# Row maxima of both heads together from the first slot on, and a new order of issue, in an attention and FFN kernel

## The chip, the cores and the metric

The kernel runs on one core of a Trainium2 chip. The metric is the device time of one execution in microseconds, the median of several runs. Below, PE is the matmul engine (TensorE), DVE the vector engine, ACT the scalar engine, POOL the GpSimd engine and SP the engine that issues all DMAs here.

## The reference

Queries, keys and values have 4 batches, 8 heads, 768 tokens and 64 columns. Each query and key is hashed to 6 bits, the signs of its products with `proj`; a query sees the keys with the same bits. The attention's output, 3072 tokens of 512 columns, goes through a feed-forward layer with 2048 hidden columns.

```python
q_bits = (np.einsum('bhsd,dk->bhsk', q, proj) > 0).astype(np.int64)
k_bits = (np.einsum('bhsd,dk->bhsk', k, proj) > 0).astype(np.int64)
...
mask = q_bucket[:, :, :, None] == k_bucket[:, :, None, :]
scores = scale * np.matmul(q, k.transpose(0, 1, 3, 2))
scores = np.where(mask, scores, -1000000000.0)
scores = scores - np.max(scores, axis=-1, keepdims=True)
attn = np.exp(scores)
attn = attn / (np.sum(attn, axis=-1, keepdims=True) + 1e-09)
return np.matmul(attn, v).astype(np.float32)
...
h = x @ w_in
sp = np.where(h > 20.0, h, np.log1p(np.exp(np.minimum(h, 20.0))))
g = h * np.tanh(sp)
return (g @ w_out).astype(np.float32)
```

## The kernel before

**Units and slots.** The work is cut into 12 units of 256 tokens, three to a batch. A unit's attention has 8 slots: four pairs of heads, and for each pair two chunks of 128 queries. There are 96 slots. Slot n makes the scores of two heads (128 queries by 768 keys each), and its steps are:

- *Scores* (`att_front`, line 841): matmuls of a slice of QT with KT into `ps_s`, a PSUM tile of 128 x 1536, 768 columns for each head. Two sums add up: one over the high halves, one over the low halves together with the hash bits, which are scaled so that keys of another bucket come out far below the others. The operations are called S, and T for the second head where heads are apart.
- *Row maximum* (line 846): DVE reduces the scores, and two small instructions (lines 850 and 853) make the scale and the bias of the exponential from it.
- *Exponential* (`att_exp`, line 873): one ACT instruction for each head, from `ps_s` into one of three buffers `pb`; it also sums the row.
- *Back* (`att_back`): the sums' reciprocal (lines 897, 903). In the first unit, PE multiplies the exponentials by a diagonal matrix (`pe_turn`, line 435), which scales and transposes them in one step, and ACT or DVE copies the result to PT (line 438). In later units the scaled exponentials are split in a high and a low float16 half (lines 366 to 369, 387, 393, 394) and transposed by DMA (line 447).
- *Output* (`att_pv`): after every second slot, PT times VT into `ps_t` (line 950 in the first unit, 939 later), and a copy to X.

**The feed-forward layer.** Each unit has 8 pieces of 256 hidden columns: H (line 985 in the first unit, 995 to 997 later), the activation on ACT (lines 1012 and 1016), a split in halves, and two matmul groups O for the two chunks of 128 tokens (line 1034, later 1044 to 1046). It trails the attention by 12 slots (`LAG`), so that the first H follows slot 10's scores. Until then the program is in its lead-in: attention of the first unit and of three slots of the second, and what prepares it.

**Preparation.** Loads of q, k, v and weights are issued by SP (line 443). Squares of them are summed on ACT (line 455) and over partitions on PE (lines 471, 472), which gives a power of two to scale by; the scaled values are split in halves, transposed by DMA (line 447) into QT and KT, hashed by PE (line 705) and DVE (lines 709, 713), and transposed again with the bits. Weights arrive as 64-bit words in a few staging regions and are brought to float32 by four steps a piece (`w_prep`: `w_u`, `w_sign`, `w_low`, `w_join`, the last at line 580).

**What sets the order.** `Plan` records every operation with the engines that could do it. The string `ORDER` names all of them by number, in the order in which they are issued, and a letter picks the engine where there is a choice. Each engine works through its own operations in that order, and waits for whatever it reads or overwrites. `BACKBONE` sets the order in which operations are numbered.

**By head.** In slots 0 to 8 (`n < BY_HEAD`, with `BY_HEAD` 9) scores and maxima are separate operations for each head: S and a maximum over one head, T and a maximum over the other. From slot 9 on, one operation S makes both heads' scores, and one reduction makes both maxima.

Of the kernel before, what the change touches and what calls it, by code (L numbers as in the profile page):

```python
# [87 lines left out]
13 7 12 6 50 15 48 52 4 34 3 97 144 77 0 1 2 20 8 17 16 14 54 53 5 21 22 35b 18 19 25 37 23c 26 9 10 11 24c 61  # L88
62 63 89 107 98c 108 99b 38 58 59 60 109c 64 27 28 36 65 66 39 29 145b 110 30 87 40 49 41 31 32 42 90 100 43
44 146 78 79c 51 46 33 147 111 67 68 69 70 163 164 165 71 72 166b 167 168 80b 45 93 91 94 92 96 95 116c 373b  # L90
55 101 81 82 126 154 83 84 214c 88 85 73 117 118 127 124 102 56 114 57 103 203c 155b 121b 119 122 74 156b 125
104 157 105 75 129 204b 128 120 130d 131 132 148 86 140 141 115 138 149 150 169 47 106 123 133 230b 143 112
185 139 134 142 183 113 151 186 205 135 231b 359 162 136 175d 176 177 184 232b 360 178 361 233 206 137 187 158
161 179 188 264b 197 212 189c 198 152 190 191c 194c 180b 213 362b 253 207 234 199 215 200 192 202 181 201 170
226 364 171 172 173 238 153 211 237 174 210 159 224 193b 182 216d 254b 255 217 218b 221b 195 225 227 160 228
196 304b 305b 219 247 222 208 248 229 239c 220 249 240 297 241c 209 244 280 315 251 306b 242 274 262 250 256
252 266d 275 307 267 257 223 281b 263 243 282b 276 277 245 235 278 246 271 268 269 236 308 279 270 289c 283
# [12 lines left out]
600 611 606 612d 622b 594 613 607 561 614 582 633 623 629 627 635 624b 583 584 630b 636 671 667 637 593 585  # L110
# [105 lines left out]

# [971 lines left out]
```

## Time and profile before

| | us |
|---|---|
| median of 3 runs | 870.38 (868.37 to 870.57) |
| the profiled execution | 869.01 |
| its span, first to last instruction | 867.2 |
| first scores start | 29.61 |
| scores of slot 9 start | 105.10 |
| first matmul of the feed-forward layer | 115.08 |
| last matmul ends | 863.4 |

All times on the trace count from the span's start. A row of a timeline gives start, duration, engine, line, instruction, what it writes and reads, how many instructions were merged, and in brackets how long its engine had been idle before it and what released it. A row of a group gives the count, then total busy time and the mean in ns of one, then the idle time before them.

### The profile page before, as it was taken

Reading aid. Unit: us, or ns where it says so; the run is one execution under the profiler, and the core shown is the slowest. Engines: PE = TensorE matmul, PEld = TensorE weight load, DVE = VectorE, ACT = ScalarE, POOL = GpSimd, SP = SyncE. Lnnn points to the kernel's source line nnn. Section 1 sums busy time; section 2 is a strip of 40 time slices with the busy share of each in tenths; the row PEclk is TensorE's granted clock in tenths of the full one; section 3 lists DMA queues with packets and bytes.
Section 4 is the critical chain, followed back from the end, with each engine's and each line's share of the span. In section 5 each row is a group of like instructions: output and inputs, shape, how many; then the busy total and the mean of one; then the engine's idle time right before and its main releaser. Section 6 shows DMA issues by size and latency. Waiting matters only on the chain. (4 is left out here: it accounts for less than half of the span.)

```text
span 867.2 us, 16893 instructions
## 1 busy us (share of the span) xinstructions
PE 804.3 (93%) x6496; PEld 549.9 (63%) x6496; DVE 650.0 (75%) x1281; ACT 616.3 (71%) x965; POOL 299.2 (35%) x286
## 2 busy tenths in 40 slices
PE   3368799999999999999999999999999999999998
PEld 1156566757657667666655757666666776676674
DVE  4556799999898887688778787678889877758331
ACT  5566889999777777667878567778977755777310
POOL 5223413334334435334430246333433424214000
PEclk9579999999999999999999999999999999999999
DMA  8966668999999877698998887979999878655400
GB/s 247 248 144 162 184 157 212 195 181 190 199 209 188 164 155 123 111 176 160 232 157 183 168 147 148 141 155 173 235 180 165 141 111 155 102 103 97 95 25 25
DMA packets 407602, 137.44 MB, mean 158 GB/s; under 512 B 377824, under 2 KB 398304, under 8 KB 407520
## 3 DMA queue, kind: packets, MB, share of 16 engines
q1 hardware_dynamic: 407520, 136.35, 79.5%
q8 instruction: 51, 0.84, 0.4%
q14 instruction: 31, 0.25, 0.1%
HBM read 35.65 MB, written 6.29 MB: 48 GB/s over the span
## 5 line engine op out<-in xcount | busy, mean ns | idle before, releaser
L873 ACT ACTIVATE pb<-ps_s,svb 128x768 f32<-128x768 f32 x192 | 189.0, 987 | 101.7 <-DVE svb L853 71.3
L846 DVE TENSOR_REDUCE svb<-ps_s 128x2 f32<-128x1536 f32 (+1 forms) x105 | 169.7, 1616 | 58.3 <-PE ps_s L841 49.4
L995 PE MATMUL ps_acc<-X,wo 128*128 128x256 f16 x616 | 167.9, 273 | 1.1 <-ACT ffb L1016 1.1
L996 PE MATMUL ps_acc<-X,wo 128*128 128x256 f16 x616 | 167.9, 273 | 0.0
L997 PE MATMUL ps_acc<-X,wo 128*128 128x256 f16 x616 | 167.9, 273 | 0.0
L841 PE MATMUL ps_s<-KT,QT 128*128 128x256 f16 (+1 forms) x768 | 145.2, 331 | 23.0 <-ACT pb L873 18.5
L387 DVE SCALAR_TENSOR_TENSOR hl<-pb,svb,hl 128x768 f16<-128x768 f32 x132 | 137.3, 1049 | 10.9 <-ACT hl L368 5.2
L1046 PE MATMUL ps_o<-wi,ffb 128*128 128x512 f16 x352 | 133.4, 379 | 0.3 <-DVE ffb L387 0.3
L1044 PE MATMUL ps_o<-wi,ffb 128*128 128x512 f16 x352 | 133.6, 379 | 0.0
L1045 PE MATMUL ps_o<-wi,ffb 128*128 128x512 f16 x352 | 133.4, 379 | 0.0
L841 PEld LDWEIGHTS <-QT 128*128 128x128 f16 x768 | 73.7, 98 | 77.3 <-issue 32.9
L366 POOL TENSOR_SCALAR hl<-pb,svb 128x768 f16<-128x768 f32 x59 | 59.7, 1014 | 142.5 <-DVE svb L903 67.6
L939 PE MATMUL ps_t<-PT,VT 128*64 128x256 f16 x1584 | 95.4, 274 | 1.0 <-DMA PT<-hl 1.0
L939 PEld LDWEIGHTS <-VT 128*64 128x64 f16 x1584 | 83.2, 110 | 17.8 <-issue 17.2
L387 DVE SCALAR_TENSOR_TENSOR ffb<-ffb,smalls 128x512 f16<-128x512 f32 x88 | 69.8, 802 | 21.9 <-ACT ffb L368 11.1
L366 POOL TENSOR_SCALAR ffb<-ffb,smalls 128x512 f16<-128x512 f32 (+1 forms) x37 | 32.7, 887 | 149.0 <-ACT ffb L1016 145.1
L1016 ACT ACTIVATE ffb<-ps_acc,smalls 128x512 f32<-128x512 f32 x88 | 58.9, 684 | 34.3 <-PE ps_acc L997 33.7
L368 ACT ACTIVATE hl<-pb,svb 128x768 f16<-128x768 f32 x67 | 61.8, 929 | 25.6 <-DMA PT<-hl 11.1
L394 POOL TENSOR_TENSOR hl<-pb,hl 128x768 f16<-128x768 f32 x44 | 74.5, 1693 | 3.7
L873 ACT ACT_TABLE_LOAD x45 | 57.7, 1283 | 20.1 <-DVE svb L853 19.1
L393 POOL TENSOR_SCALAR pb<-pb,svb 128x768 f32<-128x768 f32 x44 | 43.9, 998 | 80.2 <-ACT hl L368 43.2
L996 PEld LDWEIGHTS <-wo 128*128 128x128 f16 x616 | 60.3, 98 | 12.9 <-issue 1.4
(203 smaller groups left out, 1272.8 us busy)
## 6 DMA issues: line engine op xcount, KB each, us to landing
out_dram<-ffb SPq DMA_DIRECT2D x24, 256.0 KB, 2.8
stg<-in_v_dram SPq DMA_DIRECT2D x13, 384.0 KB, 4.2
stg<-in_k_dram SPq DMA_DIRECT2D x12, 384.0 KB, 4.2
wo<-in_q_dram SPq DMA_DIRECT2D x9, 512.0 KB, 5.2
stg<-in_moe_w_in_dram SPq DMA_DIRECT2D x8, 512.0 KB, 4.6
stg<-in_moe_w_out_dram SPq DMA_DIRECT2D x6, 512.0 KB, 4.7
PT<-hl SPq DMA_TRANSPOSE x176, 4.0
wo<-in_moe_w_out_dram SPq DMA_DIRECT2D x5, 512.0 KB, 4.9
```

Of the source, the lines that this page charges most:

```text
L366: POOL=lambda: nc.gpsimd.tensor_scalar(out=dst, in0=src, scalar1=sc, scalar2=1.0, op0=ALU.mult, op1=ALU.mult),
L387: return [("DVE", 215 + 1.035 * n, port(lambda: nc.vector.scalar_tensor_tensor(out=dst, in0=src, scalar=sc, in1=hi, op0=ALU.mult, op1=ALU. ...
L841: nc.tensor.matmul(ps_s[:, hh * S + c0 * P:hh * S + c1 * P], QTb[:, u % 2, sl, qi], KTb[:, j, sl, hh * NCH + c0:hh * NCH + c1].rearrange(" ...
L846: nc.vector.tensor_reduce(out=sv[:, 0, lo:hi], in_=ps_s[:, lo * S:hi * S].rearrange("p (h e) -> p h e", e=S), axis=AX.X, op=ALU.max, negat ...
L873: EXP[n, hh] = op("exp", [("ACT", 1075, lambda hh=hh, t=t: nc.scalar.activation(pb[:, t], ps_s[:, hh * S:(hh + 1) * S], AF.Exp, bias=sv[:, ...
L939: nc.tensor.matmul(pv[hh * D:(hh + 1) * D, 0:256], vt[:, w, hh * NCH + c], pt[:, hh, a * NCH + c].rearrange("p s t -> p (s t)"), start=(x ...
L995: nc.tensor.matmul(o, wh, X[:, 0, c], start=(c == 0), stop=False)
L996: nc.tensor.matmul(o, wh, X[:, 1, c], start=False, stop=False)
L997: nc.tensor.matmul(o, wl, X[:, 0, c], start=False, stop=(c == NCC - 1))
L1044: nc.tensor.matmul(PS[f"o{s}"], gh, wh, start=first, stop=False)
L1045: nc.tensor.matmul(PS[f"o{s}"], gh, wl, start=False, stop=False)
L1046: nc.tensor.matmul(PS[f"o{s}"], gl, wh, start=False, stop=last)
```

## The change

`BY_HEAD` becomes 0, so that all 96 slots issue both heads' scores as one operation and reduce both rows in one instruction. That is 18 operations fewer (9 scores, 9 maxima), of 2601. The operations are numbered anew, and `ORDER` is another string: all operations stand in a new order, and some are done by another engine. The program's text is one line shorter, so the line numbers of the new kernel are one lower.

```diff
 ORDER = """
-13 7 12 6 50 15 48 52 4 34 3 97 144 77 0 1 2 20 8 17 16 14 54 53 5 21 22 35b 18 19 25 37 23c 26 9 10 11 24c 61
...
-2596b 2600 2597
+12 7 6 8 17 138 3 13 0 5 4 77 1 2 9 10 18 19 23c 25 20 21 22 52 64 35b 34 95 36 11 87 37c 50 48 16 15 49 51 58
...
+2571 2574 2573 2566 2576 2575 2530 2570 2580 2581b 2582 2577 2578b 2579
 """
...
-KV_PE, Q_PE, BY_HEAD = 1, 1, 9
+KV_PE, Q_PE, BY_HEAD = 1, 1, 0
```

DVE around slots 2 and 3, before: the reductions (`svb<-ps_s`) are by head, 128x1 each, and the first row is head 1 of slot 2.

```order
L846 TENSOR_REDUCE svb<-ps_s 128x1
L850 TENSOR_SCALAR svb<-svb,smalls 128x1
L853 TENSOR_TENSOR svb<-svb 128x1
L709 TENSOR_REDUCE hsum<-ps_t 128x72
L846 TENSOR_REDUCE svb<-ps_s 128x1
L850 TENSOR_SCALAR svb<-svb,smalls 128x1
L853 TENSOR_TENSOR svb<-svb 128x1
L476 TENSOR_SCALAR hw<-ps_t 128x1
L460 TENSOR_SCALAR smalls<-hw 128x1
L713 TENSOR_SCALAR wo<-hsum 128x12x6
L846 TENSOR_REDUCE svb<-ps_s 128x1
```

The same place after the change, from slot 2's one reduction on (`wo<-wo` at L579 is a weight's last step, `stg<-stg` and `wo<-stg` are steps of the next weight):

```order
L845 TENSOR_REDUCE svb<-ps_s 128x2
L849 TENSOR_SCALAR svb<-svb,smalls 128x2
L852 TENSOR_TENSOR svb<-svb 128x2
L579 SCALAR_TENSOR_TENSOR wo<-wo 128x1024
L712 TENSOR_SCALAR wo<-hsum 128x12x6
L368 TENSOR_SCALAR stg<-stg 128x1024
L475 TENSOR_SCALAR smalls<-ps_t 128x4
L459 TENSOR_SCALAR smalls<-smalls 128x4
L560 TENSOR_SCALAR wo<-stg 128x1024
L902 RECIPROCAL svb<-svb 128x2
L817 TENSOR_SCALAR smalls<-smalls 128x1
L761 TENSOR_SCALAR smalls<-smalls 128x4
```

Slot 3's one reduction stands two rows further on. In each slot one reduction of two heads takes the place of two of one, and weight steps stand between them that stood elsewhere or on other engines.

SP at the start, before: from the loads ahead of the first pair of transposes (Q and K, high and low halves) to the second pair (low halves with hash bits).

```order
L443 DMA stg<-in_moe_w_in_dram 128x2x512
L443 DMA wi<-in_v_dram 128x2x384
L443 DMA wo<-in_moe_w_out_dram 128x1024
L443 DMA stg<-in_v_dram 128x2x384
L447 DMA_TRANSPOSE QT<-tok_64 128x16x128
L447 DMA_TRANSPOSE KT<-wo 128x12x128
L443 DMA wi<-in_v_dram 128x2x384
L443 DMA hl<-in_v_dram 128x2x384
L443 DMA X<-in_q_dram 128x8x128
L447 DMA_TRANSPOSE QT<-tok_65 128x16x128
L447 DMA_TRANSPOSE KT<-wo 128x12x128
```

SP at the same place after the change:

```order
L442 DMA stg<-in_moe_w_in_dram 128x2x512 x2
L442 DMA wi<-in_v_dram 128x2x384
L442 DMA hl<-in_v_dram 128x2x384
L446 DMA_TRANSPOSE QT<-tok_64 128x16x128
L446 DMA_TRANSPOSE KT<-wo 128x12x128
L442 DMA wi<-in_v_dram 128x2x384
L442 DMA stg<-in_v_dram 128x2x384
L446 DMA_TRANSPOSE QT<-tok_65 128x16x128
L446 DMA_TRANSPOSE KT<-wo 128x12x128
L442 DMA X<-in_q_dram 128x8x128
```

The half weight `wo<-in_moe_w_out_dram` and the second unit's queries `X<-in_q_dram` moved behind the second pair of transposes.

More of the change, by code (lines that the diff above doesn't have):

```diff
@@ L93 @@
[L93 to L97, printed above, removed]
@@ L198 @@
[L198 to L201 removed]
+12 7 6 8 17 138 3 13 0 5 4 77 1 2 9 10 18 19 23c 25 20 21 22 52 64 35b 34 95 36 11 87 37c 50 48 16 15 49 51 58
+26 27 61 28 38 62 105b 63 65 39b 24b 66 96c 59 60 29 40 14 53 30 32 89 31 41 42 33 44 43 45 91 106b 107b 108
@@ new lines @@
+411 525 473 495b 491 492b 488 496b 449 478 527 450 480 497c 451 498 489 437 439 352 481 583 428 490 503 493
+494 511c 512 513c 429 532 528 545 544 533b 499 479 520b 515b 529 514 535 482 502 521 534 522b 536c 517 504c
+530 551 461 505 537 462 506b 523 507 516 483 518 585 500 578 550 552 584 508 586 553 546 538b 540 554 570d 501
+547 646 548c 549 587 556 555 590 602 608 539 542 571 541 616 543 591b 557 558 588 579b 573 592 589 559 560
+561b 572b 574b 593 594d 575 580 474 649 576b 563 581b 475 595 582 597b 596 562 604b 611 603 509 653 638 612b
@@ new lines @@
+1223 1192b 1195b 1234 1206 1207 1225 1235 1251c 1194 1196 1224b 1266 1262 1208c 1187 1227 1252 1270 1282 1226
+1188 1228 1054 1210b 1155 1211 1271 1267 1263 1264b 1254 1253c 1156 1255 1257 1272 1273 1287 1288 1283 1284
+1265 1209 1274 1275 1278 1297 1199 1279 1238 1239 1289b 1268 1291b 1256 1258 1298b 1259 1260 1229 1240 1290c
+1293 1241 1285c 1242c 1286 1244 1296 1212 1382 1292 1299 1230 1213 1300 1316 1317 1276b 1319 1215 1214 1327
+1328 1269 1277 1322 1294 1245 1216 1295 1332 1325 1318b 1320b 1329 1330 1337d 1338 1333 1346 1386 1334 1280
@@ new lines @@
+2160 2140 2150 2215 2344 2151 2169b 2161c 2216 2054b 2125 2143 2142 2065 2153 2176 2180 2172 2152 2154 2156
+2170 2171 2165c 2166 2162 2183 2184 2218 2193 2145 2194b 2144 2155 2186c 2185c 2187 2157 2177 2173 2174 2181
+2182 2189 2178c 2195 2196 2197c 2198 2199 2192 2191 2206 2205 2175 2208 2209b 2201b 2211 2188 2207 2226 2225
+2219 2190 2200c 2203 2179 2257 2202 2204 2210 2227 2229b 2228 2230 2231b 2240 2241b 2242 2217b 2232b 2235b
+2233 2243 2258 2262 2266 2237 2220 2267 2244d 2245 2221 2238b 2259 2080 2236 2234 2263 2260c 2264 2268 2246c
@@ new lines @@
+2248 2252 2270 2278 2269 2247c 2250 2261 2249 2251 2281b 2223 2282 2283c 2291 2274 2279 2271 2253 2275 2292
+2285 2265 2222 2289 2290 2303 2304 2284c 2287 2276 2272 2224 2286 2288 2294 2293 2280 2273 2295b 2296 2306
+2307b 2308 2297b 2299 2305 2311 2310 2298c 2301 2300 2302 2309 2314 2315 2316c 2323 2318b 2324b 2312 2313
+2317b 2319 2336 2340 2320 2325 2326 2277 2327b 2328 2329 2337 2331 2345 2346 2321 2332 2239 2357 2341 2347
+2348 2358 2349 2335 2353 2322 2330c 2333b 2342b 2343 2334 2370 2360 2338c 2361 2359 2339 2363 2366 2362c 2371
@@ new lines @@
+2354 2350 2355 2351 2356 2364 2352 2369 2368 2390 2372 2373 2365 2374c 2375 2377 2376b 2378b 2382 2385 2384
+2383 2401 2389 2386b 2387 2391 2392 2367 2388 2393 2394 2395 2380 2404 2379 2397b 2381 2416 2419 2423 2398
+2405 2396b 2407 2406 2408 2409 2410 2402b 2399 2427 2411b 2412b 2420 2424 2425b 2439 2431 2435 2428 2430 2429
+2442 2421 2422 2426 2414b 2413 2400 2415 2254 2443 2444b 2452 2432 2436 2450 2497 2501 2453b 2454 2445c 2446
+2448b 2417b 2455 2433b 2447 2437b 2440 2434 2456c 2457 2459 2467 2458c 2441 2460b 2468b 2469 2451 2472 2464
```

192 lines of the change are left out of this document (85 added, 107 removed).

## Prediction

> **What bounds the kernel now.** I read the page's head first, then the windows by stage, then the chain of waits inside the stage that stood out, and last the timeline of single slots in it.
>
> ```profile
> span 867.2 us, 16893 instructions
> PE 804.3 (93%) x6496; PEld 549.9 (63%) x6496; DVE 650.0 (75%) x1281; ACT 616.3 (71%) x965; POOL 299.2 (35%) x286
> ```
>
> PE is busy for 804.3 of 867.2 us, so at most 63 us are there to be won without taking work from PE. The windows say where they lie (columns: window, then busy time of PE, PEld, DVE, ACT, POOL with instruction counts, granted clock, DMA share, GB/s).
>
> ```profile
> 0.00:29.60 29.60, 8.28 (x56) 4.51 (x57) 13.02 (x39) 17.34 (x31) 13.55 (x18) 0.86 0.90 247
> 29.60:115.10 85.50, 60.46 (x447) 43.96 (x446) 55.70 (x127) 57.03 (x97) 27.04 (x31) 0.85 0.72 178
> 115.10:200.00 84.90, 84.50 (x517) 57.29 (x516) 82.18 (x148) 80.18 (x123) 25.60 (x23) 1.00 0.88 184
> 200.00:863.50 663.50, 651.10 (x5484) 444.14 (x5482) 498.35 (x971) 461.72 (x716) 233.06 (x214) 1.00 0.80 149
> ```
>
> The first cut is at the first scores (29.6), the second at the first FFN matmul (115.1). Behind 115.1 PE has work nearly all the time: 84.50 + 651.10 = 735.6 of 748.4 us, 12.8 idle. Between the two cuts it idles for 25.0 of 85.5 us, and so do DVE (29.8) and ACT (28.5): no engine is full there, so a chain of waits sets the length. FFN work cannot fill it, since the first FFN matmul needs the outputs of slots 0 to 7. What was waited for in that stretch (us in total, times, longest):
>
> ```profile
> PE ps_s L841 <- ACT pb L873: 14.5, 10, 2.7
> PE ps_s L841 <- DVE svb L846: 3.2, 3, 1.1
> DVE svb L846 <- PE ps_s L841: 14.5, 9, 3.2
> ```
>
> The chain is scores, row maximum, exponential, next scores. Here are slots 2 and 3 on PE, ACT and DVE:
>
> ```profile
> 49.60 0.81 PE L841 MATMUL ps_s<-KT,QT 128*128 128x512 f16 x4 [1.12 <-DVE svb L846]
> 53.35 0.81 PE L841 MATMUL ps_s<-KT,QT 128*128 128x256 f16 x4 [1.19 <-ACT pb L873]
> 56.90 1.44 PE L841 MATMUL ps_s<-KT,QT 128*128 128x512 f16 x4 [2.73 <-ACT pb L873]
> ...
> 52.22 0.99 ACT L873 ACTIVATE pb<-ps_s,svb 128x768 f32<-128x768 f32 x1 [1.58 <-PE ps_l L435]
> 55.76 0.99 ACT L873 ACTIVATE pb<-ps_s,svb 128x768 f32<-128x768 f32 x1 [1.77 <-DVE hw L476]
> ...
> 54.27 0.96 DVE L846 TENSOR_REDUCE svb<-ps_s 128x1 f32<-128x768 f32 x1 [3.23 <-PE ps_s L841]
> 58.44 0.96 DVE L846 TENSOR_REDUCE svb<-ps_s 128x1 f32<-128x768 f32 x1 [2.41 <-PE ps_s L841]
> ```
>
> The reader is to see that the heads do not run beside each other. Head 0's scores of slot 2 are the row at 49.60, done at 50.41. Their maximum starts at 54.27, 0.11 us after the *other* head's scores of slot 3 ended (53.35 + 0.81 = 54.16). Head 1's maximum of slot 3 starts at 58.44, after the scores at 56.90, which are head 0's. So the order by heads is one serial chain, head after head: from scores at 53.35 to scores at 56.90 are 3.55 us, 7.10 for a slot's two heads.
>
> The trace shows the wait, not its reason. The Trainium skill has one, in "PSUM — Partial Sum Buffer", section "PSUM bank collisions raise a hardware error": accesses of two engines must be kept apart by bank and quadrant, not by address. ps_s is three banks of 512 for two heads of 768, so by that rule both share the middle one. By a rule of addresses a head would cost 3.55 us beside the other, and fusing would lose 9 x (6.1 - 3.55) = 23 us, an estimate; the trace agrees with the rule of banks.
>
> A slot with both heads in one, as every slot from 9 on is now, looks like this where nothing delays it:
>
> ```profile
> 665.28 1.46 PE L841 MATMUL ps_s<-KT,QT 128*128 128x512 f16 x8
> 666.78 1.76 DVE L846 TENSOR_REDUCE svb<-ps_s 128x2 f32<-128x1536 f32 x1
> 668.57 0.23 DVE L850 TENSOR_SCALAR svb<-svb,smalls 128x2 f32<-128x2 f32 x1
> 668.84 0.16 DVE L853 TENSOR_TENSOR svb<-svb 128x2 f32<-128x2 f32 x1
> 669.09 0.99 ACT L873 ACTIVATE pb<-ps_s,svb 128x768 f32<-128x768 f32 x1 [0.32 <-DVE svb L853]
> 670.08 0.98 ACT L873 ACTIVATE pb<-ps_s,svb 128x768 f32<-128x768 f32 x1
> 671.36 0.81 PE L841 MATMUL ps_s<-KT,QT 128*128 128x512 f16 x4
> ```
>
> From scores to scores: 671.36 - 665.28 = 6.08 us.
>
> **The change part by part.** *Matmuls.* The fused slot has the same eight, so PE's work is unchanged in sum; its cost is nothing.
>
> *The slots of the lead-in.* Now they take this long:
>
> ```profile
> 29.61 0.80 PE L841 MATMUL ps_s<-KT,QT 128*128 128x256 f16 x2
> 105.10 1.46 PE L841 MATMUL ps_s<-KT,QT 128*128 128x512 f16 x8
> 110.97 2.81 PE L950 MATMUL ps_t<-PT,stg 128*64 128x256 f32 x24 [1.67 <-issue]
> 113.72 1.47 PE L841 MATMUL ps_s<-KT,QT 128*128 128x512 f16 x8
> 115.08 1.11 PE L985 MATMUL ps_acc<-X,wi 128*128 128x256 f32 x4
> ```
>
> Nine slots from 29.61 to 105.10: 75.49 us, 8.39 each, of which 7.10 is the serial chain. With fused slots the chain is 6.08; it is the lower end, 8.39 the upper. What can hold a slot above 6.08 is DVE, whose other work must fit between two maxima:
>
> ```profile
> L846 DVE TENSOR_REDUCE svb<-ps_s 128x1 f32<-128x768 f32 x18 | 17.2, 954 | 21.5 <-PE ps_s L841 14.5 <-ACT ffb L368 2.9 <-ACT wi L573 2.3
> L853 DVE TENSOR_TENSOR svb<-svb 128x1 f32<-128x1 f32 x18 | 5.0, 279 | 0.6
> L850 DVE TENSOR_SCALAR svb<-svb,smalls 128x1 f32<-128x1 f32 x18 | 3.9, 214 | 0.6
> L387 DVE SCALAR_TENSOR_TENSOR tok<-X,smalls,tok 128x1024 f16<-128x1024 f32 x2 | 2.6, 1284 | 0.8 <-ACT tok L368 0.8
> L387 DVE SCALAR_TENSOR_TENSOR VT<-wi,smalls,VT 128x768 f16<-128x768 f32 x1 | 1.0, 1014 | 0.0
> L580 DVE SCALAR_TENSOR_TENSOR wo<-stg,wo 128x1024 int32<-128x1024 int32 x1 | 1.2, 1224 | 0.0
> L369 DVE TENSOR_SCALAR wi<-wi 128x1024 f32<-128x1024 f32 x1 | 0.7, 696 | 0.1
> ```
>
> By head the maxima cost 18 x (0.954 + 0.279 + 0.214) = 26.0 us; fused, 9 x (1.76 + 0.23 + 0.16) = 19.4, so 6.6 less. Against that the new order puts about 14 us more on DVE between first scores and FFN: a weight join (1.2) and two residual subtracts (1.3 + 1.0) that stood ahead of the first scores, five scalings and five sign steps of weights that POOL or ACT had (10 x 0.7), two subtracts (2.0) and small ones. So DVE has 55.7 - 6.6 + 14 = 63 us there, ACT 57 + 4 (six squares came in, weight casts and scalings went out) and PE 60.5: at least 63 us for a stretch of 85.5. Spread over nine slots and the piece behind them, DVE asks 2.15 for the maximum and 3.5 to 4.7 for other work in each, 6.3 on average, while the chain leaves it 6.08 - 2.15 = 3.9. Some slots are DVE's, others the chain's, and PE's in-order transposes and outputs delay some. I take 7.1, between the two floors (6.08, 6.3) and 8.39, nearer to the floors because the largest wait of the rows above has no counterpart in the new order. 9 x (8.39 - 7.1) = 11.6 us earlier; bounds 0 and 20.8.
>
> *The first scores.* They wait for the transposes of Q and K, the second pair of which is queued on SP behind loads (the issue of Q's took 5.50 us for that):
>
> ```profile
> 22.22 5.50 SPq L447 DMA_TRANSPOSE QT<-tok  x1
> 31.57 2.08 PE L841 MATMUL ps_s<-KT,QT 128*128 128x256 f16 x6 [1.16 <-DMA KT<-wo]
> X<-in_q_dram SPq DMA_DIRECT2D x2, 512.0 KB, 5.5
> ```
>
> Ahead of K's, fifteen loads stand on SP before the change and thirteen after it; the two that went behind (a weight half and the second unit's Q) have 512 KB each, 1.05 MB together, at the 247 GB/s of the first window 4.2 us. Against it, that Q's squares still stand on ACT ahead of the first exponential, and its load (5.5 us to landing) is now issued behind the K transpose; it holds the first exponentials, not the first scores. I take 3 us earlier; bounds 0 and 6.
>
> *Ninth slot to FFN.* 115.08 - 105.10 = 10.0 us, fused already, with the same two outputs and last transposes: no change.
>
> *Behind the first FFN matmul.* The same matmuls, and by the order about as much work of DVE, ACT and POOL stands behind it as before, so nothing was pushed past the cut: DVE was busy 82.2 of 84.9 us there and has no room. Its waits are new: 12.8 us idle now, bounds -6 and +8, value 0. The nine or so subtracts that go from DVE to POOL are covered by PE; without that cover each would cost its slot a late transpose.
>
> Sum: -11.6 - 3 = -14.6 us. The profiled execution took 869.0, the median of the runs is 870.38, 1.4 more; 870.4 - 14.6 = 855.8.
>
> **The rivals.** *Partial gain.* Late weight loads or in-order transposes hold slots at 7.7: 6.2 us from the slots and little from the start, 863. For it: the DMA share is 0.72 in that stretch, and the same transfers in 85.5 - 11.6 = 73.9 us make 0.83.
>
> *No gain.* The one fused pair in the lead-in now, 105.10 to 113.72, took 8.62 us, no less than 8.39. If all ten do, the time stays at 868 to 873. Against it: two attention outputs (2.81 us for the second, and an idle 1.67 before it) stood between those two, and the new order has one at most between any two slots.
>
> *Half clock, slower.* The granted clock is 0.85 in the lead-in and 1.00 behind. PE's 60.46 us there are 51.4 at full clock and 102.8 at half; were the clock 0.5 throughout, PE itself would take 103 us instead of 85.5, and even with 3 us won at the start the time would be 870.4 + 17.3 - 3 = 885. It decides from a mean clock of 51.4 / 88.5 = 0.58 downward. Against it: PE holds the same work in less time, so its busy share rises. This is what the Trainium skill's "TensorE: Matmul & The Clock Gate", Part 1, gives for an engine with idle gaps: half rate is the default, and about 3.4 us of sustained work release it. By that rule the maxima's gaps could leave PE cold; the 0.85 beside a share of 71% speaks against.
>
> *Given back, slower.* New waits behind 115 double the 12.8 us and the slots gain little: 875. PE's long busy stretch speaks against it.
>
> **How the numbers follow.** A measurement tells about 0.3% (2.6 us) from no change. Chances: forecast (848 to 860) 0.58; more than that 0.05; partial (860 to 867) 0.20; no gain 0.08; half clock 0.03; given back 0.06. So faster 0.83, same 0.08, slower 0.09. The predicted time is the forecast's. The range takes in the partial case and most of the bounds of the two terms: 848 to 867.
>
> **What would show it.** Right: the reduce at L845 no longer waits several microseconds for PE; slots 0 to 9 start 6.5 to 7.5 us apart; the first FFN matmul stands near 100 us; PE idles 10 to 15 us behind it. The first scores should come at 26 to 28. Wrong: slots still 8 us apart with DVE waiting for DMA-fed weights; a clock near 0.5 up to 100 us; or PE gaps behind the first FFN matmul well over 13 us.

## The result, and the profile after

The kernel after takes 836.21 us, the median of 4 runs (835.91 to 838.14); the kernel before took 870.48 beside it (868.37 to 872.84, 4 runs). The ratio is 0.961, with a 95% interval of 0.9582 to 0.9639. The forecast was 855.8 with a range of 848 to 867: the direction was right, and the gain is more than twice the forecast's.

The head of the page of after's profiled execution, which took 838.14 us, the longest of the four:

```profile
span 836.4 us, 16885 instructions
PE 799.6 (96%) x6496; PEld 548.4 (66%) x6496; DVE 655.5 (78%) x1267; ACT 603.9 (72%) x944; POOL 322.5 (39%) x300
```

PE has the same 6496 matmuls and is busy for 4.7 us less; the span is 30.8 us shorter. The windows of after by stage (columns as in the prediction). The cuts are the start of the first scores (21.2), slots 3 and 9 (51.01 and 86.91), the first FFN matmul (94.71) and the end of the last matmul (832.55):

```profile
21.20:94.71 73.51, 56.88 (x454) 42.04 (x451) 61.95 (x128) 55.74 (x98) 26.74 (x28) 0.86 0.87 217
51.01:86.91 35.90, 33.76 (x290) 26.10 (x290) 33.26 (x75) 33.62 (x58) 10.95 (x14) 1.00 0.74 187
94.71:832.55 737.84, 734.19 (x5999) 501.75 (x5997) 582.54 (x1111) 536.22 (x828) 284.74 (x257) 1.00 0.83 157
```

The same cuts of before:

```profile
53.35:105.10 51.75, 38.10 (x278) 29.22 (x278) 32.60 (x76) 37.03 (x66) 14.74 (x18) 0.90 0.52 137
115.08:863.43 748.35, 735.62 (x5999) 501.45 (x5997) 580.52 (x1116) 541.93 (x838) 258.66 (x237) 1.00 0.81 153
```

Two things are to be seen. Slots 3 to 8 took 51.75 us, and PE idled for 13.6 of them; now they take 35.90, and PE, DVE and ACT are all busy for 33 to 34 of them. And behind the first FFN matmul PE idled for 12.7 us, and now for 3.7. The first FFN matmul comes 20.4 us earlier (115.08 to 94.71), and what follows is 10.5 us shorter (748.35 to 737.84): 30.9 us in sum, the 30.9 between the two profiled executions (869.01 and 838.14).

Slot 5 and the start of slot 6 in the timeline of after (the rows of the slot's chain alone):

```profile
62.96 1.46 PE L840 MATMUL ps_s<-KT,QT 128*128 128x512 f16 x8
64.46 1.76 DVE L845 TENSOR_REDUCE svb<-ps_s 128x2 f32<-128x1536 f32 x1
66.25 0.23 DVE L849 TENSOR_SCALAR svb<-svb,smalls 128x2 f32<-128x2 f32 x1
66.51 0.16 DVE L852 TENSOR_TENSOR svb<-svb 128x2 f32<-128x2 f32 x1
66.71 0.99 ACT L872 ACTIVATE pb<-ps_s,svb 128x768 f32<-128x768 f32 x1
67.69 0.98 ACT L872 ACTIVATE pb<-ps_s,svb 128x768 f32<-128x768 f32 x1
68.90 0.81 PE L840 MATMUL ps_s<-KT,QT 128*128 128x512 f16 x4
```

From scores to scores are 5.94 us. Each step starts within 0.25 us of the end of the one before it, although all three engines are busy for more than nine tenths of slots 3 to 8. That is the bare chain.

What PE waited for behind the first FFN matmul, first before, then after (us in total, times, longest):

```profile
PE ps_s L841 <- ACT pb L873: 3.9, 7, 1.6
PE ps_t L705 <- DMA KT<-tok: 3.0, 4, 1.6
PE ps_t L471 <- ACT tok L455: 1.8, 2, 1.0
PE ps_acc L995 <- ACT ffb L1016: 1.1, 1, 1.1
```

```profile
PE ps_s L840 <- ACT pb L872: 1.1, 4, 0.5
PE ps_t L470 <- DVE X L964: 0.8, 1, 0.8
PE ps_acc L994 <- ACT ffb L1015: 0.6, 2, 0.4
```

It is no single wait that went. Scores waiting for exponentials, hashes for transposes (L705) and sums of squares for ACT (L471) all shrank or disappeared.

### The profile page after: what moved, and what is told of

Same layout as the page of the kernel before. It is cut to its first block, busy times and chain, and to the rows that moved or that the text cites. A ratio compares the mean times of both kernels' runs of the same rounds, so it can differ in the third digit from the quotient of the medians.

```text
span 836.4 us, 16885 instructions
## 1 busy us (share of the span) xinstructions
PE 799.6 (96%) x6496; PEld 548.4 (66%) x6496; DVE 655.5 (78%) x1267; ACT 603.9 (72%) x944; POOL 322.5 (39%) x300
## 4 chain that ended last, share of the span: by engine, by line
PE 52%; DVE 2%; ACT 2%; DMA 1%; issue 1%; POOL 1%; SPq 0%; ACTq 0%; POOLq 0%; DVEq 0%
PE ps_s L840 8%; PE ps_o L1043 7%; PE ps_o L1045 7%; PE ps_o L1044 7%; PE ps_t L938 6%; PE ps_acc L994 6%; PE ps_acc L995 6%; PE ps_acc L996 6%; DVE svb L845 1%; ACT pb L872 1%; DMA PT<-hl 1%; DMA wo<-in_q_dram 1%; PE ps_t L704 1%; DVE hl L386 0%; SPq L446 0%
## 5 line engine op out<-in xcount | busy, mean ns | idle before, releaser
L845 DVE TENSOR_REDUCE svb<-ps_s 128x2 f32<-128x1536 f32 x96 | 168.5, 1755 | 42.1 <-PE ps_s L840 37.2
L840 PE MATMUL ps_s<-KT,QT 128*128 128x512 f16 (+1 forms) x768 | 144.2, 331 | 12.3 <-DMA KT<-wo 7.9
L386 DVE SCALAR_TENSOR_TENSOR hl<-pb,svb,hl 128x768 f16<-128x768 f32 x123 | 129.6, 1059 | 7.0 <-ACT hl L367 4.4
L840 PEld LDWEIGHTS <-QT 128*128 128x128 f16 x768 | 73.7, 99 | 68.1 <-issue 18.7
L365 POOL TENSOR_SCALAR hl<-pb,svb 128x768 f16<-128x768 f32 x67 | 67.9, 1013 | 116.6 <-DVE svb L902 52.3
L393 POOL TENSOR_TENSOR hl<-pb,hl 128x768 f16<-128x768 f32 x53 | 89.2, 1683 | 4.4
L392 POOL TENSOR_SCALAR pb<-pb,svb 128x768 f32<-128x768 f32 x53 | 54.4, 1027 | 91.4 <-DVE hl L368 43.3
L386 DVE SCALAR_TENSOR_TENSOR ffb<-ffb,smalls 128x512 f16<-128x512 f32 x88 | 68.0, 783 | 20.3 <-ACT ffb L367 18.9
L367 ACT ACTIVATE hl<-pb,svb 128x768 f16<-128x768 f32 x62 | 57.2, 929 | 17.5 <-DMA PT<-hl 8.8
L995 PEld LDWEIGHTS <-wo 128*128 128x128 f16 x616 | 60.2, 98 | 12.0 <-issue 1.3
L994 PEld LDWEIGHTS <-wo 128*128 128x128 f16 x616 | 60.2, 98 | 11.3 <-issue 2.0
```

Of the source, the lines that this page charges most:

```text
L386: return [("DVE", 215 + 1.035 * n, port(lambda: nc.vector.scalar_tensor_tensor(out=dst, in0=src, scalar=sc, in1=hi, op0=ALU.mult, op1=ALU. ...
L393: nc.gpsimd.tensor_tensor(out=dst, in0=src, in1=hi, op=ALU.subtract)
L840: nc.tensor.matmul(ps_s[:, hh * S + c0 * P:hh * S + c1 * P], QTb[:, u % 2, sl, qi], KTb[:, j, sl, hh * NCH + c0:hh * NCH + c1].rearrange(" ...
L845: nc.vector.tensor_reduce(out=sv[:, 0, lo:hi], in_=ps_s[:, lo * S:hi * S].rearrange("p (h e) -> p h e", e=S), axis=AX.X, op=ALU.max, negat ...
L994: nc.tensor.matmul(o, wh, X[:, 0, c], start=(c == 0), stop=False)
L995: nc.tensor.matmul(o, wh, X[:, 1, c], start=False, stop=False)
```

## The experiments

Every kernel below computes all of the reference. The table gives the median, the ratio to the kernel before on the same chip with its 95% interval, and from each profiled execution the start of the first FFN matmul and the time from there to the end of the last matmul.

| kernel | us | ratio | first FFN matmul | behind it |
|---|---|---|---|---|
| before | 870.48 | 1 | 115.08 | 748.35 |
| after | 836.21 | 0.961 (0.9582 to 0.9639) | 94.71 | 737.84 |
| oldorder_fused | 861.50 | 0.9927 (0.9902 to 0.9952) | 108.67 | 747.17 |
| neworder_byhead | 839.82 | 0.9681 (0.965 to 0.9713) | 96.37 | 738.12 |
| newlead_oldrest | 849.92 | 0.9805 (0.9764 to 0.9845) | 92.56 | 750.33 |
| oldlead_newrest | 858.09 | 0.9897 (0.9854 to 0.9941) | 112.88 | 737.30 |
| oldorder_fused_exps | 860.12 | 0.9908 (0.9879 to 0.9937) | 107.86 | 746.34 |
| oldorder_byhead_together | 868.59 | 0.9999 (0.9979 to 1.0019) | 114.44 | 749.17 |
| neworder_interleaved | 858.08 | 0.9896 (0.9868 to 0.9923) | 114.12 | 738.01 |
| newrest_oldengines | 951.16 | 1.0963 (1.0934 to 1.0992) | 92.39 | 853.99 |
| oldrest_newengines | 965.23 | 1.1129 (1.11 to 1.1157) | 92.16 | 866.78 |
| newsp_oldloads | 837.07 | 0.9646 (0.9617 to 0.9674) | 94.24 | 737.59 |
| improved1 | 835.19 | 0.9629 (0.9604 to 0.9654) | 92.63 | 737.40 |
| before_gaps | 888.94 | 1.023 (1.0186 to 1.0273) | 118.23 | 766.22 |
| oldorder_newchain | 875.99 | 1.0085 (1.0054 to 1.0116) | 122.86 | 746.34 |
| after_again | 835.30 | 0.9621 (0.9587 to 0.9654) | 92.91 | 737.12 |
| improved2 | 847.75 | 0.9762 (0.9732 to 0.9791) | 92.74 | 749.68 |

One and the same lead-in ended at 112.9 (oldlead_newrest), 115.1 (before) and 118.2 (before_gaps) in three executions, and the new one between 92.2 and 94.7 in five. So in that column differences under 3 us between kernels with the new lead-in are not read, nor those under 6 us between kernels with the old one. The last column is steadier: 746.3 to 750.3 with the old order behind the first FFN matmul, 737.1 to 738.1 with the new.

Diffs that only renumber `ORDER` are shown by the operations' names: S and T as in the description of the kernel, `max`, `exp` and `tp` (the turn at line 435) with the slot and, behind a dot, the head.

### Fusing, or the order

Four kernels take the change apart. Theory A is the prediction's: one chain for two heads instead of one each makes the gain in the lead-in. Theory B is that the order makes it. Theory C is that what came behind the first FFN matmul belongs to the order there, theory D that it is a consequence of the lead-in.

**oldorder_fused**: before's order and engines, slots 0 to 8 fused.

```diff
-KV_PE, Q_PE, BY_HEAD = 1, 1, 9
+KV_PE, Q_PE, BY_HEAD = 1, 1, 0
-S5 max5.0 max5.1 exp5.0 S6 max6.0 exp5.1 T6 exp6.0
+S5 max5 exp5.0 exp5.1 S6 max6 exp6.0 exp6.1
```

> The order and the engines of before, but in slots 0 to 8 the two score operations become one, at the place of the later of the two, and so do the two maxima; an operation that would then come ahead of what it needs is held back to the first place where it can stand. Theory A (the chain by heads cost the lead-in its 20 us): the first FFN matmul comes near 103, 12 us earlier than before, since slots fall from 8.4 to about 7, and the time is 855 to 861. Rival B (the new order and its engines shortened the lead-in, fusing did nothing): the first FFN matmul stays near 115 and the time at 868 to 872.

**neworder_byhead**: after's order and engines, slots 0 to 8 by head, with S and T side by side and the maxima side by side.

```diff
-KV_PE, Q_PE, BY_HEAD = 1, 1, 0
+KV_PE, Q_PE, BY_HEAD = 1, 1, 9
-S6 max6 exp6.0 exp6.1
+S6 T6 max6.0 max6.1 exp6.0 exp6.1
```

> The new order and engines, but in slots 0 to 8 each fused score operation is two again, one right behind the other, and each fused maximum two, one right behind the other. Theory A: the heads cannot overlap, each slot pays two reductions of 1.45 us in place of one of 2.15, 0.7 us in nine slots, so the first FFN matmul is 5 to 8 us later than in the changed kernel and the time 841 to 846. Rival B: only the order counted, 836 to 838. If heads did run beside each other when issued together, it would be faster than 836.

**newlead_oldrest** has after's order and engines up to the first FFN matmul and before's behind it; **oldlead_newrest** the reverse. The line of newlead_oldrest in which the first changed number stands:

```diff
...
-320c 354 305 298 356 321 328 345b 315 322 269 329b 270 324 333b 334 386 291 388 294 304 319 318 335 369b 330
...
+320c 354 305 298 356 321 328 345b 315 322 269 329b 270 324 333b 334 347 294 319 369 304 318 386 316 397b 323
...
```

> The changed kernel up to the first FFN matmul, and from there on what is left in the order and with the engines of before. Theory C (the idle time of PE behind the first FFN matmul, 12.8 us before and 3.2 after, belongs to the order of that part): the first FFN matmul stays at 95, the idle behind it returns to 11 to 14 us, and the time is 844 to 848. Rival D (it went because the lead-in leaves the other engines less behind, whatever the order): idle 3 to 5 us and 836 to 839.

> The kernel before, by head, up to the first FFN matmul, and from there on what is left in the new order with the new engines. Theory C: the first FFN matmul stays at 115, PE idles about 3 us behind it, and the time is 859 to 862, so that lead-in (20) and rest (10) add up. Rival D: idle stays near 12 us and the time near 869.

The two halves add up: newlead_oldrest has the early start and the old 750.3 us behind it, oldlead_newrest the old start and the new 737.3. PE idles for 13.7 of the 750.3 us and for 3.6 of the 737.3. So theory C holds in its mechanism, though both times (849.9 and 858.1) lie 1 to 2 us outside its ranges, and D fell: what came behind the first FFN matmul is the order and engines there, and does not follow from the lead-in.

In the lead-in neither A nor B holds alone. Fusing in the old order brought the first FFN matmul from 115.1 to 108.7, short of A's 103, and the time to 861.5 where A had 855 to 861 and B 868 to 872. By head in the new order it stands at 96.4 and the time at 839.8, between A's 841 to 846 and B's 836 to 838. Fusing is worth 5 us of time in the old order (861.5 beside 866.8 for before on that chip) and 4 to 6 in the new (839.8 to 836.2 by the medians, 0.9681 to 0.961 by the ratios); the new order by head, with its choice of engines, is worth 27 (866.8 to 839.8). Between the profiled executions 18.7 us of that lie in the lead-in (115.08 to 96.37) and 10.2 behind it. Order and engines in the lead-in were not tried apart.

Slot 4 of neworder_byhead shows why it costs so little to stay by head there (timeline of PE, DVE and ACT; the row at 55.73 is both heads' scores, merged):

```profile
55.73 1.46 PE L841 MATMUL ps_s<-KT,QT 128*128 128x512 f16 x8
57.22 0.96 DVE L846 TENSOR_REDUCE svb<-ps_s 128x1 f32<-128x768 f32 x1
58.54 0.95 DVE L846 TENSOR_REDUCE svb<-ps_s 128x1 f32<-128x768 f32 x1
60.05 1.00 ACT L873 ACTIVATE pb<-ps_s,svb 128x768 f32<-128x768 f32 x1 [1.06 <-DVE svb L853]
61.03 0.98 ACT L873 ACTIVATE pb<-ps_s,svb 128x768 f32<-128x768 f32 x1
```

With the heads side by side a slot goes through one chain, 6.43 us from 55.73 to the next scores at 62.16, only 0.5 more than fused. The first maximum still starts when both heads' scores are done (57.22 against 57.19), as the Trainium skill's rule of banks ("PSUM — Partial Sum Buffer", section "PSUM bank collisions raise a hardware error") has it; the wait is the program's own, and no run here shows what the chip would do without it. What costs 7.1 us a slot is then not two instructions in place of one, but the place of the other head's instructions between them.

### How the heads stand

**neworder_interleaved**: neworder_byhead with the heads interleaved over the slots, as before had them.

```diff
-S6 T6 tp5.0 max6.0 max6.1 exp6.0 exp6.1 S7 T7
+T6 exp5.0 tp4.1 S6 tp5.0 max6.1 exp6.1 T7 max6.0 exp6.0 S7
```

> The new order by head in slots 0 to 8, with the heads interleaved over the slots as before had them in slots 2, 6 and 8: the next slot's T stands ahead of this slot's second maximum, wherever what it needs stands there already. By head but side by side the first FFN matmul stood at 96.4 and slots were 6.5 us apart. Theory G: the chain goes head after head, 3.55 us each, 7.1 a slot or more; the first FFN matmul at 101 to 106, time 844 to 850. Rival H (interleaving costs nothing, and the loss before lay in the other operations of the old order): 95 to 98, time 838 to 841.

The first FFN matmul is back at 114.1, 17.8 us behind neworder_byhead and where before has it, although the two orders differ in the places of 24 operations alone: one score operation of each of the nine slots, one maximum of each, and six exponentials. The time is 858.1 where theory G had 844 to 850. Slots 3 to 8 take 8.8 us each (52.78 to 105.71). The chain of one head behind the other can be followed around slots 6 and 7 (timeline):

```profile
80.71 0.81 PE L841 MATMUL ps_s<-KT,QT 128*128 128x512 f16 x4
81.56 0.96 DVE L846 TENSOR_REDUCE svb<-ps_s 128x1 f32<-128x768 f32 x1 [0.55 <-PE ps_s L841]
83.08 0.99 ACT L873 ACTIVATE pb<-ps_s,svb 128x768 f32<-128x768 f32 x1 [1.17 <-DVE svb L853]
85.53 0.82 PE L841 MATMUL ps_s<-KT,QT 128*128 128x256 f16 x4
86.46 0.96 DVE L846 TENSOR_REDUCE svb<-ps_s 128x1 f32<-128x768 f32 x1 [3.51 <-PE ps_s L841]
87.96 0.99 ACT L873 ACTIVATE pb<-ps_s,svb 128x768 f32<-128x768 f32 x1 [2.48 <-DVE svb L853]
```

In its list of PE's waits up to the first FFN matmul one line carries nearly all:

```profile
PE ps_s L841 <- ACT pb L873: 18.7, 10, 3.4
```

In neworder_byhead that line had 4.2 us, so it makes 14.5 of the 17.8. DVE and ACT idle in turn while one head is under way. So G's cause is right in the new order, and its price was too low.

**oldorder_byhead_together** is the reverse in the old order.

```diff
-S5 max5.0 max5.1 exp5.0 S6 max6.0 exp5.1 T6 exp6.0
+S5 T5 max5.0 max5.1 exp5.0 exp5.1 S6 T6 max6.0 exp6.0 max6.1 exp6.1
```

> The old order, still by head in slots 0 to 8, but with the two heads of a slot side by side: scores S and T next to each other, then both maxima, then both exponentials. Theory G (by heads costs much only where the order lets a head of one slot stand between the two of another; side by side it costs the second maximum, 0.5 to 0.6 us a slot as in the new order by head): the first FFN matmul near 108, 7 us ahead of before's 115.1, and 5 us behind the fused order with its exponentials side by side; time 860 to 864. Theory A of the prediction (a chain of 3.55 us for each head, whatever the order): 113 to 116, time 866 to 871.

No change: 114.4, 868.6 us, where A had 113 to 116 and G 108. G, whose cause was right in the new order, fails in the old one. There, with the heads side by side, PE's waits for exponentials and maxima ahead of the first FFN matmul fall from 17.7 to 12.7 us, and its other waits grow from 13.8 to 17.7. A's number holds without its reason, since the chain from head to head is mostly gone here.

### What is left in the old order

**oldorder_fused_exps**: oldorder_fused, the exponentials of a slot side by side.

```diff
-S5 max5 exp5.0 tp4.0 tp4.1 exp5.1 S6
+S5 max5 exp5.0 tp4.0 exp5.1 tp4.1 S6
```

> The old order with slots 0 to 8 fused, as in the run oldorder_fused, where the first FFN matmul stood at 108.7; here the two exponentials of each of slots 0 to 9 also stand side by side on ACT. In that run slots 2, 3, 5 and 7 had 0.7, 1.7, 1.7 and 1.7 us of other ACT work between their exponentials, 5.8 us in all, and the next scores waited for the later one. Theory E (what is left of the lead-in's loss in the old order is what it puts between the two exponentials): the first FFN matmul near 103, time 5 to 6 us under that of oldorder_fused, 854 to 857. Rival F (the work that stood between them only moves behind them and delays the next maximum or transpose): 107 to 109, time 860 to 862.

Rival F holds: 107.9 and 860.1 us. In slots 2, 3 and 7 the exponentials did come together or nearer, and slots 4 and 8 then waited longer for their maxima (1.61 and 0.59 us in place of 0.96 and 0.04). In slot 5 they could not: there are three buffers for exponentials, and the second of slot 5 needs the one that slot 4's turn empties. oldorder_fused shows it; the row at 72.90 is two turns merged (`ps_l<-ffb,pb`), and slot 4's is the second, behind slot 5's scores and slot 3's turn:

```profile
70.96 2.14 PE L840 MATMUL ps_s<-KT,QT 128*128 128x512 f16 x8 [0.46 <-ACT pb L872]
72.90 3.85 PE L434 MATMUL ps_l<-ffb,pb 128*128 128x128 f32 x24
75.53 0.99 ACT L872 ACTIVATE pb<-ps_s,svb 128x768 f32<-128x768 f32 x1 [3.23 <-DVE ho L475]
78.22 0.99 ACT L872 ACTIVATE pb<-ps_s,svb 128x768 f32<-128x768 f32 x1
79.36 1.46 PE L840 MATMUL ps_s<-KT,QT 128*128 128x512 f16 x8 [0.37 <-ACT pb L872]
```

Slot 5 takes 8.4 us there (70.96 to 79.36), 2.5 over the bare chain. The buffer is not all of it: the turn ends at 76.75, and ACT does a weight step (L367, 77.19 to 78.35) ahead of the second exponential.

**oldorder_newchain** takes the whole attention chain of slots 2 to 9 as the new order has it, ahead of the slot's other work, and leaves that work and all engines as the old order has them.

```diff
-S5 max5 exp5.0 tp4.0 tp4.1 exp5.1 S6
+S5 max5 tp4.0 exp5.0 exp5.1 tp4.1 S6
```

> The old order with fused slots, where from slot 2 to slot 9 the operations of the attention chain (scores, maximum, exponentials, sums, reciprocals, diagonals, turns and their copies) stand among themselves as in the new order and ahead of the other work of the same slot; all other work, and every choice of engine, stays as in the old order. In the run oldorder_fused slots were 7.28 us apart and the first FFN matmul at 108.7; in the kernel after 5.98 and 94.7. Theory P (what is left is the arrangement of the chain: turns that free an exponential's buffer stand a slot late): slots of 6.0 to 6.6, the first FFN matmul at 100 to 104, time 852 to 857. Rival Q (it is the other work: too much of it on ACT between two slots): slots of 7 or more, the first FFN matmul at 106 to 110, time 858 to 863.

Neither P (100 to 104) nor Q (106 to 110): the first FFN matmul comes at 122.9, and the time is 876.0, slower than before. Slot 2 takes 6.0 us, the bare chain, and slot 3 takes 12.9. PE from slot 3's scores to slot 4's:

```profile
53.61 1.46 PE L840 MATMUL ps_s<-KT,QT 128*128 128x512 f16 x8 [1.00 <-ACT pb L872]
54.91 3.02 PE L434 MATMUL ps_l<-ffb,pb 128*128 128x128 f32 x24
61.65 0.16 PE L470 MATMUL ps_t<-smalls,ones 128*128 128x1 bf16 x1 [3.72 <-ACT tok L454]
61.67 0.16 PE L471 MATMUL ps_t<-floors,ones 128*128 128x1 bf16 x1
62.09 4.50 PE L949 MATMUL ps_t<-PT,wi 128*64 128x256 f32 x24 [0.25 <-DVE smalls L475]
```

A sum over partitions (L470), 0.16 us of work, waits for a square of the second unit's queries, which ACT now does behind the exponentials. The output (L949) and slot 4's scores, which stand behind it on PE, wait with it. Slot 6 takes 13.1 us, and there the output waits 4.08 us for a small step of DVE (L475). The chain was put first on one engine, and another engine's queue made the chain wait for its filler. In this arrangement, then, the new chain loses more with the old order's other work than it gains; whether another arrangement of that work would do, with the old engines, was not tried.

### Behind the first FFN matmul

**newrest_oldengines** is the kernel after with before's choice of engine behind the first FFN matmul; **oldrest_newengines** is newlead_oldrest with after's choice there. Each changes some 400 letters and no place in the order; the first of newrest_oldengines is 369, the first step of a weight:

```diff
-320c 354 305 298 356 321 328 345b 315 322 269 329b 270 324 333b 334 386 291 388 294 304 319 318 335 369b 330
+320c 354 305 298 356 321 328 345b 315 322 269 329b 270 324 333b 334 386 291 388 294 304 319 318 335 369 330
...
```

> The kernel after, with the old choice of engine for every operation behind the first FFN matmul that has one (400 letters of ORDER), and the new order. From the first FFN matmul to the last matmul are 748.4 us before and 737.8 after, with PE gaps of over 0.2 us of 10.9 and 3.1 us in sum. Theory I (the gain behind the first FFN matmul comes from the order): 736 to 740 for that stretch, time 835 to 839. Theory J (it comes from the choice of engines, 26 scalings and sums taken off ACT among them): 746 to 750, time 845 to 849.

> The after's order up to the first FFN matmul and the before's order behind it, as in the run newlead_oldrest, but with the new choice of engine behind it too. In newlead_oldrest the stretch from the first FFN matmul to the last matmul took 750.3 us. Theory I (the order makes the gain behind it): 748 to 752, time 846 to 850. Theory J (the engines make it): 737 to 741, time 836 to 840.

Neither theory I nor J: 854.0 and 866.8 us in place of 737.8 and 750.3. The first waits of PE behind the first FFN matmul, in newrest_oldengines and in oldrest_newengines:

```profile
PE ps_s L840 <- ACT pb L872: 55.3, 39, 4.4
PE ps_o L1045 <- DVE ffb L386: 8.0, 3, 4.8
```

```profile
PE ps_s L840 <- ACT pb L872: 57.6, 41, 4.8
PE ps_t L704 <- DVE X L964: 7.9, 5, 4.4
```

No engine got too much to do: in newrest_oldengines ACT is busy for 540.7, DVE for 598.6 and POOL for 260.3 us of those 854.0 (541.9, 580.5 and 258.7 in before). What broke is the fit: an exponential that comes late because another operation now stands ahead of it on its engine. In slot 13 of newrest_oldengines, for one, four operations of ACT stand between the two exponentials (started at 125.56 and 131.35), where after has one, and slot 14's scores wait 3.93 us for the second. So the gain can't be given to the order or to the engines alone; they are one plan.

**before_gaps** asks whether before's 12.7 us of idle PE can be had at the places where they lie. 14 operations that PE waited for are put behind the next one or two on PE, with what depends on them.

```diff
-S41 O271
+O271 S41
```

> The kernel before, with the 14 PE operations behind the first FFN matmul that PE waited over 0.25 us for (10.7 us in sum) each put behind the next one to two operations on PE, whose work is longer than the wait. Theory N (the idle behind the first FFN matmul sits in single places where PE's row stands just ahead of what it waits for): the stretch from the first FFN matmul to the last matmul shrinks from 748.4 to 738 to 742 us, time 858 to 862. Rival O (the waits come back at the next operation, since what PE waits for is late as a chain): 746 to 750, time 865 to 870.

**improved2** does the same at 9 places of the kernel improved1 (below).

> The run improved1 (the fifth transpose of K ahead of two weight halves on SP) with the 9 PE operations behind the first FFN matmul that PE waited over 0.18 us for there (3.5 us in sum) each put behind the next one to two operations on PE. Theory N: the stretch from the first FFN matmul to the last matmul shrinks from 737.4 to 734.5 to 736, time 832 to 834.5. Rival O: 737 to 739 and 835 to 837.

Both are slower: 766.2 and 749.7 us behind the first FFN matmul, 18 and 12 more. The waits come back at the next operation, as rival O said, but far larger than it had them. In before_gaps the 1.04 us that slot 41's scores had waited are gone, and slot 42's wait for 5.16 in their place:

```profile
386.47 2.72 PE L841 MATMUL ps_s<-KT,QT 128*128 128x512 f16 x8 [5.16 <-ACT pb L873]
```

The moved scores themselves are hardly later: in before they start 0.1 us behind the end of the exponential that they wait for (367.13), in before_gaps 0.3 (375.96). It is their maximum that is late, first in before, then in before_gaps:

```profile
369.11 1.75 DVE L846 TENSOR_REDUCE svb<-ps_s 128x2 f32<-128x1536 f32 x1
382.06 1.75 DVE L846 TENSOR_REDUCE svb<-ps_s 128x2 f32<-128x1536 f32 x1
```

It started 0.5 us behind the end of its scores, and now starts 4.6 us behind it. What depends on the scores was moved with them, so that the maximum now stands behind four operations of DVE (three subtracts and a step of X) that had stood behind it, and two of these wait for ACT and POOL. In improved2 the longest wait, 3.50 us, is likewise that of slot 28, behind the moved slot 27. So the price was shown for moving a place of PE with all that hangs on it; a row of PE moved alone, with the maximum kept ahead of that work, was not tried here.

### The start

**newsp_oldloads** is the kernel after with the two loads of 1.05 MB back where before issued them, ahead of the first and of the second transpose of Q.

```diff
-26 27 61 28 38 62 105b 63 65 39b 24b 66 96c 59 60 29 40 14 53 30 32 89 31 41 42 33 44 43 45 91 106b 107b 108
+26 27 61 54 28 38 62 105b 63 65 39b 24b 66 96c 59 60 29 40 14 53 30 32 89 31 41 42 46 33 44 43 45 91 106b 107b
```

> The kernel after, with two loads put back on SP where before had them: the weight half ahead of the first transpose of Q, and the second unit's queries ahead of the second. Theory K (the prediction's: 1.05 MB ahead of K's second transpose hold the first scores by up to 4.2 us): that transpose lands at 31 to 32 in place of 28.2, the scores of slot 0 end at 33 to 34 in place of 30.3, the first FFN matmul at 97 to 99, time 838 to 841. Rival L (slot 2 is held by the first unit's fifth transpose of K, which stood behind the weight half and now stands ahead of less; the start's loss is given back there): the first FFN matmul at 94 to 96, time 835 to 838.

L's numbers hold, 94.2 and 837.1 us. K's second transpose lands at 29.8 in place of 28.2 and slot 0's scores end at 32.0 in place of 30.3, so the two loads cost the start 1.6 us, not the 4.2 of their bytes. In after SP issues nothing from 7.5 to 14.5 us, and the weight half falls into that gap, at 7.72: K's first transpose is then issued only 0.7 us later (17.55 in place of 16.84), and the second, which stands behind the queries too, 1.6 (26.13 in place of 24.49). L's reason is not shown. Slot 2's scores are not held here (1.46 us), but they are not in after_again (below) either. Whether the 1.6 us are still there at the end is not shown: the time is 1.8 above after_again's 835.3, but 0.9 above after's 836.2, and the start of the first FFN matmul differs by less than is read.

**improved1** puts the fifth transpose of K (86) ahead of the two weight halves (54 and 55) and that weight's first steps (148 to 150) behind slot 2's maximum.

```diff
-78 79b 139b 80 67 68 46 140 69 70 97c 73 98b 109 157 92 110 111 141b 158 159 56 81 57 82 99 54 55 88 83 84 85
-193c 86 112 113 160 94 93 114d 74 115 75 162 122 123 100 148c 116b 117 118b 101 103 149 163 47 119 194b 195b
...
+78 79b 139b 80 67 68 46 140 69 70 97c 73 98b 109 157 92 110 111 141b 158 159 56 81 57 82 99 88 83 84 85 193c
+86 54 55 112 113 160 94 93 114d 74 115 75 162 122 123 100 116b 117 118b 101 103 163 47 119 194b 195b 120 124
...
```

> The kernel after, with the fifth transpose of K put ahead of the two weight halves on SP, and that weight's first three steps behind slot 2's maximum. In the kernel after, slot 2's scores take 4.13 us, since they wait for that transpose, landed at 44.5; slots 1 and 3 take 2.7 and 1.5. Theory L: the transpose lands at 41 to 42.5, slot 2's scores take 2.7 and everything behind comes 1.4 us earlier, the first FFN matmul at 93.3, time 834 to 836. Rival M (the moved weight steps delay slot 3, or PE is full from slot 3 on and the 1.4 us are lost in it): no change, 836 to 837.

**after_again** is the kernel after, unchanged, beside improved2.

> The kernel after, unchanged, beside improved2 on the same chip: 835 to 837 us. In its profiled execution of the first day the fifth transpose of K landed at 44.5 and slot 2's scores took 4.13 us; in three other kernels with the same lead-in it landed at 42.7 to 43.2. If that was one execution's chance, slot 2 takes 2.7 us or less here and the first FFN matmul stands at 92 to 93; if not, at 94.7.

In improved1 the transpose landed at 39.1 in place of 44.5 and slot 2's scores took 1.46 us in place of 4.13. But slot 2's scores did so in after_again without it: 1.46, with the transpose landed at 42.5 and the first FFN matmul at 92.91. The late transpose was one execution's chance, and 835.19 and 835.30 are the same time. No kernel tried here beats the kernel after.

## Why the prediction fell short

**The bound** was right. The lead-in was held by a chain of waits and not by an engine, and 20.4 of its 85.5 us went.

**The chain by head** was read rightly from the rows, 3.55 us for a head, but the cause was put into the wrong part of the change. The text holds the split into heads for the cause and fusing for the cure. In the new order split heads side by side cost 6.5 us for each of slots 3 to 8 (49.39 to 88.58 in neworder_byhead); interleaved they cost 8.8 (neworder_interleaved). Fusing without the new order gave 7.29 us for each of slots 3 to 8 (55.20 to 98.93 in oldorder_fused), nearly the 7.1 that was forecast for all. The forecast was in effect that of fusing alone. Fusing lost nothing in either order, so the loss of 23 us that followed from a rule of addresses is out.

**The slots, 7.1 us each**, are the step of the lead-in that failed. Slots 3 to 8 take 5.98 each: 15.9 us gained in those six, where 11.6 were forecast for nine. The discount rested on a floor of 6.3 us from DVE's work, and that floor was an average in the wrong place. The total was right (estimated at 63 us, 61.95 in the window above). But between the scores of slots 3 and 9 DVE has only 33.26 us, 5.5 a slot with the maximum; the rest stands ahead of slot 3, where transposes hold the scores anyway, and behind slot 9. A floor from an engine's sum has to be taken over the stretch where it is to hold. By the prediction's own marks, from the first scores to slot 9, the nine slots take 65.7 us, 7.3 each, so the number 7.1 is nearly met. That is luck: slots 0 to 2 take 9.9 each, and slots 3 to 8 go below its floor.

**The first scores, 3 us**: by its own mark this term is outside its bound of 6. The first scores start at 21.2, 8.4 us earlier, where 26 to 28 were foretold. But these are two of eight matmuls, and the other six wait for K's second transpose (slot 0, then slot 9):

```profile
21.19 0.80 PE L840 MATMUL ps_s<-KT,QT 128*128 128x512 f16 x2
28.23 2.08 PE L840 MATMUL ps_s<-KT,QT 128*128 128x512 f16 x6 [6.24 <-DMA KT<-wo]
86.91 1.47 PE L840 MATMUL ps_s<-KT,QT 128*128 128x512 f16 x8
```

The early start is therefore given back in the slots. Slot 0's scores end at 30.3, and at 33.7 before, so 3.3 us earlier; slot 3 starts 2.3 us earlier. For that end the size was right, and half of the reason: the two loads make 1.6.

**Ninth slot to FFN, no change**: 7.8 us in place of 10.0. The step says that the same two outputs stand there, while the rival "no gain" says, rightly, that the new order has one at most between two slots. The two sentences contradict each other, and the step took the wrong one.

**Behind the first FFN matmul, 0**, is the other failed step: 10.5 us came, outside the bound of 6. The argument was that DVE has no room there, from the window 115.1 to 200. But PE idled for only 0.4 us in that window (84.50 of 84.90). The idle lay behind 200, 12.4 us of 663.5, with DVE busy for 75%. The quoted rows said so: where PE waits and no engine is full, an order can take the wait away, and the bound is the whole idle time, -12.8. The runs showed that order and engines behind that matmul, without the new lead-in, take PE's idle time from 12.7 to 3.6 us (oldlead_newrest).

Of the 19.6 us between forecast and result, 10.5 are that step and 5.8 the lead-in (20.4 against 14.6). The other 3.3 are the profiled executions' own: before's lay 1.4 under its median, after's 1.9 above.

**The rivals.** The clock was 0.86 in the lead-in, not near 0.5, and nothing was given back behind it. In time, "partial gain" (863) is near oldorder_fused (861.5) and "no gain" (868 to 873) near oldorder_byhead_together (868.6), though their causes were not tested there; the new order avoided both. Of what was to show it right, the reduction at L845 waits 0.5 us or less in slots 3 to 9, as foretold; the slots are shorter than 6.5 to 7.5, the first FFN matmul is ahead of 100, and PE's idle behind it is 3.7 us, not 10 to 15.

What stays open is which rule of the plan made the 10.5 us. Shown is that they belong to order and engines behind the first FFN matmul taken together, and that two attempts to move single places by hand, 14 in the old plan and 9 in the new, lost time.

## What to carry to other kernels

Where engines work through queues in a fixed order, read a new order as a whole: bound its worth by all the idle time of the bounding engine in which no other engine is full, not by the one wait that the change is named after. Take an engine's floor only over the stretch in which it is to hold. And when a row is to be moved, look first at what must move with it on the other engines: 1 us of wait removed at one place brought 5 us at the next, since a maximum came late.

## What the runs showed of the hardware

A long stall costs more than its length, since PE runs slower behind it. Eight score matmuls take 1.46 us; behind the wait of 5.16 us above they took 2.72, and in newrest_oldengines so they do behind 3.93:

```profile
132.47 2.72 PE L840 MATMUL ps_s<-KT,QT 128*128 128x512 f16 x8 [3.93 <-ACT pb L872]
```

In oldorder_newchain the output behind a wait of 3.72 us took 4.50 where others take 2.81, and the scores behind a wait of 1.00 the usual 1.46. Over the stretch behind the first FFN matmul PE's busy time rose from 734.2 to 763.0 us in newrest_oldengines, for the same 5999 records of matmuls, at a granted clock of 0.97 in place of 1.00; these 29 us are a quarter of its loss of 116. The granted clock tells the same at the start of after (20 to 25, and 50 to 55 us):

```profile
20.00:25.00 5.00, 1.14 (x14) 0.45 (x14) 4.68 (x9) 2.22 (x5) 4.87 (x4) 0.50 1.10 263
50.00:55.00 5.00, 3.24 (x24) 2.21 (x21) 4.53 (x14) 4.51 (x9) 2.31 (x3) 1.00 1.05 193
```

The Trainium skill ("TensorE: Matmul & The Clock Gate", "Part 1: The HAM clock gate") gives about 3.4 us for the idle window behind which the rate halves. The traces agree in part. Behind the first FFN matmul of newrest_oldengines and oldrest_newengines, all 7 groups of eight score matmuls behind waits over 3.4 us took longer, six of them 2.7 us, and of the 142 behind waits under 1.4 us or none, 136 took 1.46. Of the 21 between, 13 took 1.46 and 8 more, and the length of the wait alone does not decide which: in oldrest_newengines one wait of 2.67 us halved the rate, and one of 3.38 did not.

```profile
628.79 1.46 PE L840 MATMUL ps_s<-KT,QT 128*128 128x512 f16 x8 [3.38 <-ACT pb L872]
838.91 2.72 PE L840 MATMUL ps_s<-KT,QT 128*128 128x512 f16 x8 [2.67 <-ACT pb L872]
```

The prediction used the clock only for a rival over the whole lead-in; it also acts behind single waits.
